# Attention beside a gated feed-forward on one core: value products in blocks of eight key tiles, one token buffer refilled by chunks, half of v in DRAM

## The chip, the core and the metric

The kernel runs on one core of a Trainium2 chip. The metric is the device time of one execution in microseconds (us), lower is better. The kernel before took 1323.13 us (median of three runs, 1322.75 to 1323.53).

## What is computed

For 2048 tokens `x` of width 448, the output is a mix of two blocks with a gate for each token:

```
g   = sigmoid((x * gate_w).sum(-1))
a   = softmax(q k^T * 28**-0.5) v   for 16 heads of width 28,   then @ wo
b   = (relu(x @ W_gate) * (x @ W_up)) @ W_down                  width 1792
out = g * a + (1 - g) * b
```

All inputs and the output are float32.

## The kernel before, in words

**Precision.** Most products are split: an operand is rounded to the type F32R ("high", made on ScalarE, `act_high`) and the rest ("low", a subtraction on VectorE or GpSimd, `low` and `pool_low`) is kept as a second operand. A contraction over 448 becomes eleven matmuls, `TERMS`: pairs of a weight chunk and a token chunk, where chunks 0 to 3 of the tokens are the high parts and 4 to 7 the low parts. `BY_CHUNK` is the same eleven pairs, sorted so that all pairs on one quarter of the tokens stand together. Only the value products (`pv`) are plain float32; each shows in the trace as two matmuls.

**Stages.** All five engines have their order written out by hand; each engine does its instructions in program order, and waits where an operand or a buffer is not ready.

1. *Projections* (to about 152 us). `qk` and `vproj` make k, q and v from four token blocks of 512. k and q go to DRAM (`qk_d`); v stays in the tile `V` (line 104): 128 keys x 16 key tiles x 16 heads x 32, where column 28 holds ones, which gives the softmax sums. The tokens of blocks 1 to 3, high and low, go to DRAM (`x_d`, `spill_x`). They lie in slots that later hold other things: P slots (`p_slot`, line 107, five buffers) and a Q slot. Block 0 stays in the two buffers of `x_slot` (line 113).
2. *Attention and feed-forward together* (152 to 1030 us). The work is cut into 64 rounds. A round handles `PB = 4` of the 256 pairs of a head and a key tile, and has two parts. First an order string is walked letter by letter: `s` is one score matmul (line 164, 512 queries) and its exponential on ScalarE into a P slot (line 166); `m` is two matmuls of scores laid out the other way (line 138) and a maximum over them on VectorE (line 140), for a head about one and a half ahead; `x` is one of the eleven matmuls of a gate or up half of the feed-forward (`gu_mm`, line 374). Then comes a **block** of value products for the four pairs (`pv`, line 400): sixteen products on 32 columns of the array each, four side by side, which show as 32 matmuls. Rounds 0 to 57 use `ROUND` (16 s, 8 m, 11 x: 43 matmuls, as an m is two); rounds 58 to 63 use `LATE` (16 s, 22 x). After eleven x a half is complete: a gate half is taken by `relu` on ScalarE, an up half by `spill_h`, which multiplies on VectorE and sends the tile to DRAM.
3. *The rest* (from 1030 us): the remaining 22 of 56 gate/up tiles (`gate_up`, each 22 matmuls), 56 down products (`down`, 12 matmuls each) and 16 output projections (`wout`, 11 each), interleaved by the list `todo`.

**PSUM buffers around the change.** Scores have two buffers (`s`), so a score matmul needs the exponential of two before it to be done. Maxima have two (`mx`), so an m needs the maximum of two before it. Feed-forward halves have one (`x`) up to round 57, and use `mx` in LATE.

**Between rounds** come the smaller steps: loads of k and q for a later head (SyncE's queue), `smax_end` (one transpose on TensorE, line 148, two copies on ScalarE, one subtraction on VectorE, two DMAs on GpSimd's queue) once for each head, `row_sums`, `spread` and `normalise` for a finished head. After the string, and before the block, stand the splits of the next weights (`split_f`: ScalarE, GpSimd) and their loads (`fetch_f`, SyncE's queue).

**Feed-forward tokens.** Gate/up tiles 0 to 13 read token block 0, 14 to 27 block 1, and so on. Block 1 is loaded back from `x_d` at round 24 into two buffers of its own (`att_x`), block 2 at round 40 into the `x_slot` buffers, block 3 in the last stage into two more (`pf_x`).

Of the kernel before, what the change touches and what calls it, by code (L numbers as in the profile page):

```python
# [8 lines left out]
F32 = mybir.dt.float32  # L9
F32R = mybir.dt.float32r  # L10
# [8 lines left out]
P = 128  # L19
S = 2048  # L20
D = 448
H = 16
# [13 lines left out]

LEAD = 24

PB = 4

ROUND = "smsxxsmsxsmsxmsxsmsxxsmsxsmsxxsmsxs"

LATE = "sxsxxsxsxxsxsxxsxsxxsxsxxsxsxxsxsxsxsx"

# [9 lines left out]
def gated_mix_kernel(ctx, tc, x, wq, wo, wgu, wd, out):  # L56
# [8 lines left out]
    def f32(ap):  # L65
        return ap.bitcast(F32)
# [27 lines left out]

    x_d = {(tb, r): dram.tile([P, 4, TB], F32, name=f"x_d_{tb}_{r}") for tb in range(1, NB) for r in range(2)}

    l_d = [dram.tile([NB, TB], F32, name=f"l_d_{h}") for h in range(H)]
    o_d = dram.tile([D, S], F32, name="o_d")
    wo_d = dram.tile([D, D], F32, name="wo_d")
# [1 line left out]

    stk = ctx.enter_context(ExitStack())
    vp = stk.enter_context(tc.tile_pool(name="vp", bufs=1))
    V = vp.tile([P, NK, H, 32], F32, name="V")
    K = [vp.tile([P, S], F32R, name=f"K{r}") for r in range(3)]

    def p_slot(name, dt=F32):
        return vp.tile([P, 4, TB], dt, name=name, tag="P", bufs=PB + 1)

    def q_slot(name):  # L110
        return vp.tile([P, 4, TB], F32R, name=name, tag="Q", bufs=3)

    def x_slot(name):
        return keep.tile([P, 4, TB], F32R, name=name, tag="xf", bufs=2)

    Q = {}

    def load_k(h):
        for r in range(4):
            nc.sync.dma_start(f32(K[h % 3])[DH * r:DH * (r + 1)], qk_d[r % 2, 2 * DH * h:2 * DH * h + DH, :])  # L120

    def load_q(h):
        Q[h] = q_slot(f"Q_{h}").rearrange("p j t -> p (j t)")
        for r in range(4):
            nc.sync.dma_start(f32(Q[h])[DH * r:DH * (r + 1)], qk_d[r // 2, 2 * DH * h + DH:2 * DH * (h + 1), :])
# [33 lines left out]
    def scores(i, j):  # L159
        h, kt = divmod(i, NK)  # L160
        if j == 0:
            PT[i] = p_slot(f"P_{i}")
        ps = ps_s(f"s_{i}_{j}")
        nc.tensor.matmul(ps, K[h % 3][:GD + 2, kt * P:(kt + 1) * P], Q[h][:GD + 2, j * TB:(j + 1) * TB],  # L164
                         start=True, stop=True)
        nc.scalar.activation(PT[i][:, j], ps, AF.Exp, scale=SCALE)  # L166
# [3 lines left out]
    def xf(tb, b):  # L170
        return X[tb][b // 4][:, b % 4]


    with tc.tile_pool(name="qkv", bufs=1) as pa:
# [42 lines left out]
                r.append((c, c + step, part))  # L217
            return r

        slots = {0: (x_slot, x_slot), 1: (p_slot, p_slot), 2: (p_slot, p_slot), 3: (p_slot, q_slot)}  # L220

        def x_tiles(tb):
            X[tb] = tuple(f(f"X{r}_{tb}", F32R) if f is p_slot else f(f"X{r}_{tb}") for r, f in enumerate(slots[tb]))

        def split_x(tb, raw):
            for c0, c1, xr in raw:
# [21 lines left out]
        def vproj(tb, t):  # L248
            ps = ps_any(f"v_{tb}_{t}")
            for n, (a, b) in enumerate(TERMS):  # L250
                nc.tensor.matmul(ps[:, :VC], xf(tb, b)[:, t * P:(t + 1) * P], W[:, a, 2 * D:], start=(n == 0),  # L251
                                 stop=(n == NT - 1))
            k = tb * 4 + t
            nc.scalar.activation(V[:, k, :, :DH], ps[:, :D].rearrange("p (h d) -> p h d", d=DH), AF.Copy)
            nc.scalar.activation(zt[:, k:k + 1], ps[:, D:D + 1], AF.Copy)

        for tb in range(NB - 1, -1, -1):
            x_tiles(tb)
        w0 = load_w(0)
        x0 = load_x(0, 1)  # L260
        w1 = load_w(1)
# [12 lines left out]
        gate = const.tile([P, 2, NK], F32, name="gate")  # L274
        for k in K:
            nc.gpsimd.memset(f32(k)[96:128], -1.0)
        nc.gpsimd.memset(V[:, :, :, DH:], 0.0)
        nc.gpsimd.memset(V[:, :, :, DH:DH + 1], 1.0)

        split_first(w0[0], x0)  # L280
        split_w(*w1)
# [79 lines left out]
            low(w[64:, :, 6], wr[64:, :, 3], w[64:, :, 6])  # L361
            del WR[i]

    def att_x(name):
        return att.tile([P, 4, TB], F32R, name=name, tag=name[:3], bufs=1)

    def load_x_split(tb, slot):
        X[tb] = tuple(slot(f"XF{r}_{tb}") for r in range(2))
        for r in range(2):
            nc.sync.dma_start(f32(X[tb][r]), x_d[tb, r])  # L370

    def gu_mm(ps, i, s, n):
        a, b = TERMS[n]
        nc.tensor.matmul(ps, WS[i][:, s, a], xf(i // NF, b), start=(n == 0), stop=(n == NT - 1))  # L374

    RL = {}

# [17 lines left out]
    def pv(i):  # L395
        h, kt = divmod(i, NK)
        if kt == 0:
            PO[h] = ps_o(f"po_{h}")
        for j in range(NB):
            nc.tensor.matmul(PO[h][32 * j:32 * j + 32], V[:, kt, h], PT[i][:, j], start=(kt == 0), stop=(kt == NK - 1))  # L400
        del PT[i]
        if kt == NK - 1:
            OS[h] = fe.tile([P, TB], F32, name=f"os_{h}", tag="os", bufs=2)
            nc.scalar.activation(OS[h], PO.pop(h), AF.Copy)
            LS[h] = fe.tile([P, 16], F32, name=f"ls_{h}", tag="ls", bufs=2)
            nc.gpsimd.dma_start(LS[h], OS[h][DH::32].rearrange("j (p c) -> j p c", c=16))
# [19 lines left out]
    def pack_wo():  # L426

        for j in range(4):
            nc.sync.dma_start(wo_d.rearrange("(g j d) n -> j d g n", j=4, d=DH)[j], wo[32 * j:32 * j + DH])
# [13 lines left out]
        act_high(WO[:, 6], r[:, 3])  # L443
        pool_low(WO[64:, 6], r[64:, 3], WO[64:, 6])

    NR = NI // PB
    X_ROUNDS = {24: (1, att_x), 40: (2, x_slot)}
    LAST_M = (len(maxima) - 2 * LEAD) // 8

    nxt = parts = 0  # L450
    done = (LAST_M - 1 + 2 * (NR - LAST_M)) // 2

    fetch_f(0)
    fetch_f(1)
    load_k(2)
    load_q(2)
    scores(0, NB - 1)
    for r in range(NR):
        h, q = divmod(r, NK // PB)
        order = ROUND if r < LAST_M else LATE  # L460
        todo = list(range(nxt, min(nxt + (0 if r == 0 else 1 if r < LAST_M else 2), 2 * done)))
        nxt += len(todo)
        if r in X_ROUNDS:
            load_x_split(*X_ROUNDS[r])

        if q == 0 and h and h + 2 < H:
            load_k(h + 2)
            load_q(h + 2)
        if r == 1:
            gates()  # L470
        if r == 2:
            pack_wo()
        if r < LAST_M and m in range(2 * NK, len(maxima), 2 * NK):
            smax_end(m // (2 * NK) - 1)
        if r == LAST_M:
            smax_end(H - 1)
        if h and q == 1:
            row_sums(h - 1)
            spread(h - 1)
        if h and q == 2:  # L480
            normalise(h - 1)
        ns = nx = 0
        for o in order:
            if o == "s":
                i, j = PB * r + 1 + ns // NB, ns % NB
                if i < NI:
                    scores(i, j)
                ns += 1
            elif o == "m":
                smax(m)  # L490
                m += 1
            elif nx < NT * len(todo):
                i, half = divmod(todo[nx // NT], 2)
                if nx % NT == 0:
                    ps = ps_x(f"gu_{i}_{half}") if r < LAST_M else ps_w(f"gu_{i}_{half}")[:, 0]
                gu_mm(ps, i, half, nx % NT)
                nx += 1
                if nx % NT == 0:
                    (spill_h if half else relu)(i, ps)

        ready = min(nxt + (2 if r + 1 < LAST_M else 3), 2 * done + 2)
        while parts < ready:
            split_f(parts // 2, pool_low, (parts % 2,))
            parts += 1
            if parts % 2 == 0:
                fetch_f(parts // 2 + 1)
        if r == LAST_M:
            wor = load_wo()
        for i in range(PB * r, PB * (r + 1)):
            pv(i)  # L510
            if i == NI - NK // 2:
                split_wo(wor)
    stk.close()


# [17 lines left out]
    def wout(tb, t):  # L533
        if t % 2 == 0:
            GA[tb, t // 2] = ps_w(f"wo_{tb}_{t}")
        ps = GA[tb, t // 2]
        for n, (a, b) in enumerate(TERMS):
            nc.tensor.matmul(ps[:, t % 2, :D], ON[tb][b // 4][:, b % 4, t * P:(t + 1) * P], WO[:, a], start=(n == 0),  # L538
                             stop=(n == NT - 1))
        if t == 0:  # L540
            GA[tb] = pf.tile([P, 4, D], F32, name=f"ga_{tb}", tag="ga", bufs=1)
        if t % 2:
            for u in (t - 1, t):
                k = tb * 4 + u
                nc.vector.tensor_scalar(GA[tb][:, u], ps[:, u % 2, :D], gate[:, 0, k:k + 1], None, op0=OP.mult)
# [47 lines left out]
                                               op0=OP.mult, op1=OP.add)  # L593
                (nc.sync if tb == NB - 1 else nc.gpsimd).dma_start(out[k * P:(k + 1) * P, :], y)

    def pf_x(name):
        return pf.tile([P, 4, TB], F32R, name=name, tag=name[:3], bufs=1)


    todo = [(gate_up, done), (row_sums, H - 1), (gate_up, done + 1)]  # L600
    for i in range(NB * NF):
# [6 lines left out]
        todo[n:n] = new  # L608


    before(1, (spread, H - 1))
    before(3, (normalise, H - 1))
    for tb, load, split, i in ((0, 4, 6, 9), (1, 9, 11, 14), (2, 21, 24, 28), (3, 35, 38, 42)):
        before(load, (fetch_o, tb))
        before(split, (split_o, tb, 0))
        before(split + 1, (split_o, tb, 2))
        before(i, *((wout, tb, t) for t in range(4)))
    n = todo.index((gate_up, (NB - 1) * NF))
    todo[n - 4:n - 4] = [(load_x_split, NB - 1, pf_x)]

    for i in range(4):
        fetch_d(i)
# [46 lines left out]
```

## Time and profile before

| what | value |
|---|---|
| median of three runs | 1323.13 us |
| the profiled execution: its own time | 1323.03 us |
| its span in the trace | 1321.3 us |
| granted TensorE clock | 1.0 |
| stage 0 to 152 us: TensorE / VectorE / ScalarE busy | 148.5 / 100.7 / 52.6 us |
| stage 152 to 1029.8 us: TensorE / VectorE / ScalarE busy | 877.6 / 581.4 / 642.1 us of 877.8 |
| the same stage: DMA share, rate | 28%, 77 GB/s |
| stage 1029.8 us to the end: TensorE busy | 287.2 us of 291.5 |

Busy time of TensorE counts a matmul from its start to its modelled end; a matmul of 512 columns shows 395 ns, while the next one starts some 233 ns after it. So where a stream of matmuls is dense or not is read from the distance between starts, which the timeline gives, and not from the busy share. The weight loads of the matmuls are listed as an engine of their own, PEld.

### The profile page before, as it was taken

To read this page: it belongs to the slowest core of one execution; us is meant where nothing else is said; L and a number is where in the kernel's file an instruction comes from. 1 tells how busy PE (TensorE), PEld (TensorE's weight loads), DVE (VectorE), ACT (ScalarE), POOL (GpSimd) and SP (SyncE) were. 2 spreads that over 40 slices of the span, in tenths; PEclk is the share of its full clock that TensorE was granted. 3 is DMA by queue.
4 is the path that set the end of the run, shared out by engine and by line. 5 is a ranking of instruction groups with operands and counts; after the bars stand their busy time and mean duration, and the time that the engine had idled before them with its cause. 6 is when DMAs were issued, how large, how long until landed. Compare 5 with 4: busy or idle time off the path is not lost.

```text
span 1321.3 us, 17544 instructions
## 1 busy us (share of the span) xinstructions
PE 1313.3 (99%) x6689; PEld 894.3 (68%) x6689; DVE 815.3 (62%) x859; ACT 772.6 (58%) x1454; POOL 307.0 (23%) x434
## 2 busy tenths in 40 slices
PE   9999999999999999999999999999999999999998
PEld 5888656656656566566566566565655788888997
DVE  6567867767767767677677677677600456633342
ACT  5212667767767777777677677677788332322121
POOL 3111112131121212222221221312325332301120
PEclk9999999999999999999999999999999999999999
DMA  8744622313223151331324313231122674433432
GB/s 298 263 171 180 175 62 61 81 48 99 56 71 88 40 152 57 89 88 40 88 86 123 77 51 81 61 92 32 50 91 79 209 265 149 163 121 120 133 113 78
DMA packets 50013, 144.67 MB, mean 109 GB/s; under 512 B 9544, under 2 KB 16648, under 8 KB 44808
## 3 DMA queue, kind: packets, MB, share of 16 engines
q1 hardware_dynamic: 33640, 96.70, 25.5%
q0 software_dynamic: 16288, 46.84, 10.2%
q8 instruction: 53, 0.87, 0.3%
q14 instruction: 32, 0.26, 0.1%
HBM read 99.96 MB, written 43.93 MB: 109 GB/s over the span
## 4 chain that ended last, share of the span: by engine, by line
PE 98%; DMA 1%; ACT 0%; DVE 0%; issue 0%; SPq 0%; ACTq 0%
PE gu L374 22%; PE s L164 20%; PE sm L138 19%; PE po L400 17%; PE acc L586 10%; PE qk L242 4%; PE v L251 3%; PE wo L538 3%; DMA xr<-x 1%; DMA qk_d<-st 1%; PE mt L148 0%; ACT X L81 0%; DVE X L87 0%; ACT st L81 0%; ACT P L166 0%
## 5 line engine op out<-in xcount | busy, mean ns | idle before, releaser
L140 DVE TENSOR_REDUCE mx<-sm 128x1 f32<-128x1024 f32 x512 | 606.5, 1219 | 174.9 <-PE sm L138 171.9
L166 ACT ACTIVATE P<-s 128x512 f32<-128x512 f32 x1024 | 583.1, 596 | 168.6 <-PE s L164 109.3
L164 PE MATMUL s<-Q,K 114*128 114x512 f32 x1024 | 419.5, 410 | 0.5 <-ACT P L166 0.5
L138 PE MATMUL sm<-K,Q 112*128 112x512 f32 x1024 | 323.4, 399 | 0.2
L164 PEld LDWEIGHTS s<-Q,K 114*128 114x128 f32 x1024 | 192.1, 188 | 146.8 <-ACT P L166 83.1
L374 PE MATMUL gu<-XF,wg 128*128 128x512 f32 x924 | 270.8, 395 | 0.0
L400 PE MATMUL po<-P,V 128*32 128x512 f32 x2048 | 233.0, 595 | 0.0
L138 PEld LDWEIGHTS sm<-K,Q 112*128 112x128 f32 x1024 | 189.6, 189 | 45.6 <-DVE mx L140 9.9
L374 PEld LDWEIGHTS gu<-XF,wg 128*128 128x128 f32 x924 | 174.6, 189 | 34.1 <-issue 0.8
L90 POOL TENSOR_TENSOR wg<-wgr,wg 128x384 fp32r<-128x384 f32 (+1 forms) x105 | 95.8, 914 | 283.3 <-ACT wg L81 187.5
L400 PEld LDWEIGHTS po<-P,V 128*32 128x32 f32 x2048 | 60.0, 109 | 131.0 <-issue 130.7
L586 PE MATMUL acc<-WD,hh 128*128 128x448 f32 x672 | 141.7, 367 | 0.0
L586 PEld LDWEIGHTS acc<-WD,hh 128*128 128x128 f32 x672 | 126.2, 188 | 12.8
L389 POOL DMA_DIRECT2D h_d<-h x56 | 31.4, 562 | 394.6 <-DVE h L383 188.4
L383 DVE TENSOR_TENSOR h<-gu,rl 128x512 f32<-128x512 f32 x56 | 38.4, 686 | 132.1 <-ACT rl L380 71.1
L380 ACT ACTIVATE rl<-gu 128x512 f32<-128x512 f32 x56 | 33.3, 594 | 128.0 <-PE gu L374 128.0
L374 PE MATMUL gu<-X,wg 128*128 128x512 f32 x308 | 108.0, 395 | 0.0
L87 DVE TENSOR_TENSOR hh<-hr,hh 128x512 fp32r<-128x512 f32 x56 | 55.3, 988 | 51.8 <-ACT hh L81 51.8
L81 ACT ACTIVATE hh<-hr 128x512 fp32r<-128x512 f32 x56 | 35.1, 628 | 74.3 <-PE acc L586 72.4
L242 PE MATMUL qk<-X,W 128*128 128x512 f32 x308 | 76.5, 398 | 1.9 <-ACT X L81 1.6
L81 ACT ACTIVATE wg<-wgr 128x384 fp32r<-128x384 f32 x168 | 72.6, 484 | 0.0
L242 PEld LDWEIGHTS qk<-X,W 128*128 128x128 f32 x308 | 57.4, 189 | 18.0 <-ACT X L81 2.6
(56 smaller groups left out, 596.6 us busy)
## 6 DMA issues: line engine op xcount, KB each, us to landing
wgr<-wgu SPq DMA_DIRECT2D x56, 512.0 KB
qk_d<-st POOLq DMA_DIRECT2D x28, 512.0 KB, 3.7
K<-qk_d SPq DMA_DIRECT2D x64, 224.0 KB
Q<-qk_d SPq DMA_DIRECT2D x64, 224.0 KB
h_d<-h POOLq DMA_DIRECT2D x56, 256.0 KB, 2.3
hr<-h_d SPq DMA_DIRECT2D x56, 256.0 KB
x_d<-X POOLq DMA_DIRECT2D x6, 1024.0 KB, 5.1
XF<-x_d SPq DMA_DIRECT2D x6, 1024.0 KB
```

What stands on the lines that cost most here:

```text
L81: nc.scalar.activation(dst, src, AF.Copy)
L87: nc.vector.tensor_tensor(dst, src, f32(high), op=OP.subtract)
L90: nc.gpsimd.tensor_tensor(dst, src, f32(high), op=OP.subtract)
L138: nc.tensor.matmul(ps[:, c, :], Q[h][:GD, u * P:(u + 1) * P], K[h % 3][:GD, k0:k0 + TB], start=True, stop=True)
L140: nc.vector.tensor_reduce(MX[h][:, 2 * u + half:2 * u + half + 1], ps, axis=AX.XY, op=OP.max)
L164: nc.tensor.matmul(ps, K[h % 3][:GD + 2, kt * P:(kt + 1) * P], Q[h][:GD + 2, j * TB:(j + 1) * TB], start=True, stop=True)
L166: nc.scalar.activation(PT[i][:, j], ps, AF.Exp, scale=SCALE)
L242: nc.tensor.matmul(ps, W[:, a, c * P:(c + 1) * P], xf(tb, b), start=(n == 0), stop=(n == NT - 1))
L251: nc.tensor.matmul(ps[:, :VC], xf(tb, b)[:, t * P:(t + 1) * P], W[:, a, 2 * D:], start=(n == 0), stop=(n == NT - 1))
L374: nc.tensor.matmul(ps, WS[i][:, s, a], xf(i // NF, b), start=(n == 0), stop=(n == NT - 1))
L400: nc.tensor.matmul(PO[h][32 * j:32 * j + 32], V[:, kt, h], PT[i][:, j], start=(kt == 0), stop=(kt == NK - 1))
L586: nc.tensor.matmul(ACC[tb][t][:, :D], hh[:, a, t * P:(t + 1) * P], WD[:, f, b], start=(f == 0 and n == 0), stop=(f == NF - 1 and n == 2))
```

## The change

- The order strings are new. Two rounds of four pairs (`SHORT`, the old `ROUND`; the first without x, the second with one half) are followed by 28 rounds of **eight** pairs: 25 of `LONG` (32 s, 16 m, 33 x: 97 matmuls, three halves), in runs of nine, eight and eight, and after each run one of `WIDE` (32 s, 16 m, 44 x: 108 matmuls, four halves). Six rounds of `LATE` follow as before. So there are 36 blocks instead of 64, and 100 halves (50 gate/up tiles) in this stage instead of 68 (34 tiles); the last stage keeps 6 `gate_up` instead of 22.
- Nine P slots (`NP = 9`) instead of five. Two of them (5 and 6) lie in the tile `V`, which is laid out by groups of four heads now: the last two groups, heads 8 to 15, are sent to DRAM (`v_d`) as they are made, by eight DMAs on GpSimd's queue, and loaded over the first two groups when heads 0 to 3, and 4 to 7, are done (SyncE's queue, at pairs 64 and 128).
- The feed-forward's tokens have one pair of buffers. `gu_mm` goes by `BY_CHUNK`; in the last up half of a token block, when the last matmul on a quarter of the tokens has been issued, two DMAs on SyncE's queue load this quarter of the next block over it. The three separate loads and their buffers go.
- The small steps between rounds are called every four pairs as before, so every second time in the middle of a string.
- In the last stage, `spread`, `normalise`, the loads and splits of the attention output and `wout` stand at other places of the list, and `ga` has two buffers.

```diff
-PB = 4
-ROUND = "smsxxsmsxsmsxmsxsmsxxsmsxsmsxxsmsxs"
+SHORT = "smsxxsmsxsmsxmsxsmsxxsmsxsmsxxsmsxs"
+LONG = "ssmmxsxxsxsmxxsxsmsxxsxxsmmsxxsxxsxsmsxxsmsmsxsxxsxmsmsxxxxsmxssxxmsxsmsxxsmsxmss"
+WIDE = "msxxsmsxsxmsxxsxmsxxxxmssmxsxxsxxsmxmssxxxxsxsmsmsxxxxsxsmsxmsxxsxxxsmsmxxxsxsxxxsxmssxmxxss"
 LATE = "sxsxxsxsxxsxsxxsxsxxsxsxxsxsxxsxsxsxsx"
+ROUNDS = [(SHORT, 0), (SHORT, 1)] + [(LONG, 3)] * 9 + ([(WIDE, 4)] + [(LONG, 3)] * 8) * 2 + [(WIDE, 4)] + [(LATE, 2)] * 6
+NP = 9
...
+    v_d = {g: dram.tile([P, NK, 4, 32], F32, name=f"v_d_{g}") for g in (2, 3)}
...
-    V = vp.tile([P, NK, H, 32], F32, name="V")
+    V = vp.tile([P, 4, NK, 4, 32], F32, name="V")
-    def p_slot(name, dt=F32):
-        return vp.tile([P, 4, TB], dt, name=name, tag="P", bufs=PB + 1)
+    def p_slot(k, name, dt=F32):
+        if k in (5, 6):
+            return V[:, k - 3].rearrange("p k h d -> p (k h d)").rearrange("p (j t) -> p j t", t=TB)
+        return (vp if k < 5 else att).tile([P, 4, TB], dt, name=name, tag=f"P{k}", bufs=1)
...
+            if t == 3:
+                for g in (2, 3):
+                    nc.gpsimd.dma_start(v_d[g][:, k - 3:k + 1], V[:, g, k - 3:k + 1])
...
-        nc.gpsimd.memset(V[:, :, :, DH:], 0.0)
-        nc.gpsimd.memset(V[:, :, :, DH:DH + 1], 1.0)
+        for g in range(G):
+            nc.gpsimd.memset(V[:, g, :, :, DH:], 0.0)
+            nc.gpsimd.memset(V[:, g, :, :, DH:DH + 1], 1.0)
...
+    for tb in range(1, NB):
+        X[tb] = X[0]
     def gu_mm(ps, i, s, n):
-        a, b = TERMS[n]
+        a, b = BY_CHUNK[n]
         nc.tensor.matmul(ps, WS[i][:, s, a], xf(i // NF, b), start=(n == 0), stop=(n == NT - 1))
+        c = b % 4
+        if i % NF == NF - 1 and s and i < NB * NF - 1 and (n == NT - 1 or BY_CHUNK[n + 1][1] % 4 != c):
+            for r in range(2):
+                nc.sync.dma_start(f32(X[0][r])[:, c], x_d[i // NF + 1, r][:, c])
...
+    def small_things(u):
+        h, q = divmod(u, 4)
+        if q == 0 and h and h + 2 < H:
+            load_k(h + 2)
+            load_q(h + 2)
+        if u in (16, 32):
+            g = u // 16 + 1
+            nc.sync.dma_start(V[:, g % 2], v_d[g])
...
+        if h and q == 1:
+            row_sums(h - 1)
+            spread(h - 1)
+        if h and q == 2:
+            normalise(h - 1)
...
-    for r in range(NR):
+    for r, (order, nu) in enumerate(ROUNDS):
+        ni = order.count("s") // NB
...
+        small_things(i0 // 4)
+        if m % (2 * NK) == 0 and i0 <= NI - LEAD:
             smax_end(m // (2 * NK) - 1)
...
+                i, j = i0 + 1 + ns // NB, ns % NB
+                if ns == 4 * NB:
+                    small_things(i0 // 4 + 1)
...
-        for i in range(PB * r, PB * (r + 1)):
+        for i in range(i0, i0 + ni):
             pv(i)
...
-    before(1, (spread, H - 1))
-    before(3, (normalise, H - 1))
-    for tb, load, split, i in ((0, 4, 6, 9), (1, 9, 11, 14), (2, 21, 24, 28), (3, 35, 38, 42)):
+    before(0, (spread, H - 1))
+    before(1, (normalise, H - 1))
+    for tb, load, split, at in ((0, 2, 3, (4, 5, 6, 7)), (1, 5, 8, (10, 11, 14, 14)), (2, 21, 24, (28,) * 4),
+                                (3, 35, 38, (42,) * 4)):
```

More of the change, by code (lines that the diff above doesn't have):

```diff
@@ L113, in x_slot @@
     def x_slot(name):
-        return keep.tile([P, 4, TB], F32R, name=name, tag="xf", bufs=2)
+        return keep.tile([P, 4, TB], F32R, name=name, tag=name[:2], bufs=1)
     Q = {}
@@ L161, in scores @@
         if j == 0:
-            PT[i] = p_slot(f"P_{i}")
+            PT[i] = p_slot(i % NP, f"P_{i}")
         ps = ps_s(f"s_{i}_{j}")
@@ L218, in load_x @@
             return r
-        slots = {0: (x_slot, x_slot), 1: (p_slot, p_slot), 2: (p_slot, p_slot), 3: (p_slot, q_slot)}
-        def x_tiles(tb):
-            X[tb] = tuple(f(f"X{r}_{tb}", F32R) if f is p_slot else f(f"X{r}_{tb}") for r, f in enumerate(slots[tb]))
+        X[0] = tuple(x_slot(f"X{r}") for r in range(2))
+        free = iter(range(5))
+        for tb in range(NB - 1, 0, -1):
+            X[tb] = tuple(q_slot(f"X{r}_{tb}") if tb + r == NB else p_slot(next(free), f"X{r}_{tb}", F32R)
+                          for r in range(2))
         def split_x(tb, raw):
@@ L253, in vproj @@
             k = tb * 4 + t
-            nc.scalar.activation(V[:, k, :, :DH], ps[:, :D].rearrange("p (h d) -> p h d", d=DH), AF.Copy)
+            nc.scalar.activation(V[:, :, k, :, :DH], ps[:, :D].rearrange("p (g h d) -> p g h d", g=G, d=DH), AF.Copy)
             nc.scalar.activation(zt[:, k:k + 1], ps[:, D:D + 1], AF.Copy)
-        for tb in range(NB - 1, -1, -1):
-            x_tiles(tb)
+            if t == 3:
+                for g in (2, 3):
+                    nc.gpsimd.dma_start(v_d[g][:, k - 3:k + 1], V[:, g, k - 3:k + 1])
         w0 = load_w(0)
@@ L362, in split_f @@
             del WR[i]
[L364 to L370, printed above, removed]
+    for tb in range(1, NB):
+        X[tb] = X[0]
     def gu_mm(ps, i, s, n):
-        a, b = TERMS[n]
+        a, b = BY_CHUNK[n]
         nc.tensor.matmul(ps, WS[i][:, s, a], xf(i // NF, b), start=(n == 0), stop=(n == NT - 1))
+        c = b % 4
+        if i % NF == NF - 1 and s and i < NB * NF - 1 and (n == NT - 1 or BY_CHUNK[n + 1][1] % 4 != c):
+            for r in range(2):
+                nc.sync.dma_start(f32(X[0][r])[:, c], x_d[i // NF + 1, r][:, c])
     RL = {}
@@ L399, in pv @@
         for j in range(NB):
-            nc.tensor.matmul(PO[h][32 * j:32 * j + 32], V[:, kt, h], PT[i][:, j], start=(kt == 0), stop=(kt == NK - 1))
+            nc.tensor.matmul(PO[h][32 * j:32 * j + 32], V[:, h // 4 % 2, kt, h % 4], PT[i][:, j], start=(kt == 0),
+                             stop=(kt == NK - 1))
         del PT[i]
@@ L444, in split_wo @@
         pool_low(WO[64:, 6], r[64:, 3], WO[64:, 6])
[L446 to L451, printed above, removed]
+    done = sum(n for _, n in ROUNDS) // 2
+    nxt = parts = i0 = 0
+    def small_things(u):
[6 more added lines that the diff above has]
+            nc.sync.dma_start(V[:, g % 2], v_d[g])
+        if u == 1:
+            gates()
+        if u == 2:
+            pack_wo()
+        if h and q == 1:
[3 more added lines that the diff above has]
+            normalise(h - 1)
     fetch_f(0)
@@ L457, in gated_mix_kernel @@
     scores(0, NB - 1)
-    for r in range(NR):
[L459 to L473, printed above, removed]
-            smax_end(m // (2 * NK) - 1)
[L475 to L481, printed above, removed]
+    wor = None
+    for r, (order, nu) in enumerate(ROUNDS):
+        ni = order.count("s") // NB
+        late = "m" not in order
+        todo = list(range(nxt, nxt + nu))
+        nxt += nu
+        small_things(i0 // 4)
+        if m % (2 * NK) == 0 and i0 <= NI - LEAD:
+            smax_end(m // (2 * NK) - 1)
+        if late and wor is None:
+            wor = load_wo()
         ns = nx = 0
@@ L484, in gated_mix_kernel @@
             if o == "s":
-                i, j = PB * r + 1 + ns // NB, ns % NB
+                i, j = i0 + 1 + ns // NB, ns % NB
+                if ns == 4 * NB:
+                    small_things(i0 // 4 + 1)
                 if i < NI:
@@ L491, in gated_mix_kernel @@
                 m += 1
-            elif nx < NT * len(todo):
+            elif nx < NT * nu:
                 i, half = divmod(todo[nx // NT], 2)
                 if nx % NT == 0:
-                    ps = ps_x(f"gu_{i}_{half}") if r < LAST_M else ps_w(f"gu_{i}_{half}")[:, 0]
+                    ps = ps_w(f"gu_{i}_{half}")[:, 0] if late else ps_x(f"gu_{i}_{half}")
                 gu_mm(ps, i, half, nx % NT)
@@ L499, in gated_mix_kernel @@
                     (spill_h if half else relu)(i, ps)
-        ready = min(nxt + (2 if r + 1 < LAST_M else 3), 2 * done + 2)
+        ready = nxt + (ROUNDS[r + 1][1] if r + 1 < len(ROUNDS) else 2)
+        ready += ready % 2
         while parts < ready:
@@ L506, in gated_mix_kernel @@
                 fetch_f(parts // 2 + 1)
-        if r == LAST_M:
-            wor = load_wo()
-        for i in range(PB * r, PB * (r + 1)):
+        for i in range(i0, i0 + ni):
             pv(i)
@@ L512, in gated_mix_kernel @@
                 split_wo(wor)
+        i0 += ni
+    assert i0 == NI and m == len(maxima), (i0, m)
     stk.close()
@@ L540, in wout @@
         if t == 0:
-            GA[tb] = pf.tile([P, 4, D], F32, name=f"ga_{tb}", tag="ga", bufs=1)
+            GA[tb] = pf.tile([P, 4, D], F32, name=f"ga_{tb}", tag="ga", bufs=2)
         if t % 2:
@@ L594, in down @@
                 (nc.sync if tb == NB - 1 else nc.gpsimd).dma_start(out[k * P:(k + 1) * P, :], y)
-    def pf_x(name):
-        return pf.tile([P, 4, TB], F32R, name=name, tag=name[:3], bufs=1)
     todo = [(gate_up, done), (row_sums, H - 1), (gate_up, done + 1)]
@@ L616, in gated_mix_kernel @@
         before(split + 1, (split_o, tb, 2))
-        before(i, *((wout, tb, t) for t in range(4)))
-    n = todo.index((gate_up, (NB - 1) * NF))
-    todo[n - 4:n - 4] = [(load_x_split, NB - 1, pf_x)]
+        for t, i in enumerate(at):
+            before(i, (wout, tb, t))
     for i in range(4):
```

## The prediction

> **What bounds the kernel now.** I read the page first. TensorE is busy 99% of the span, and the chain that ended last runs on it for 98%; ScalarE and VectorE stand at 58% and 62%. But a busy share does not say that matmuls follow each other as closely as they can, so I then read the timeline of TensorE by the starts of its matmuls, around one round of the long middle stage:
>
> ```profile
> PE   9999999999999999999999999999999999999998
> ...
> PE 98%; DMA 1%; ACT 0%; DVE 0%; issue 0%; SPq 0%; ACTq 0%
> ```
> ```profile
> 599.81 0.40 PE L164 MATMUL s<-Q,K 114*128 114x512 f32 x1
> 600.13 3.64 PE L400 MATMUL po<-P,V 128*32 128x512 f32 x32
> 603.71 0.50 PE L164 MATMUL s<-Q,K 114*128 114x512 f32 x1
> 604.05 0.62 PE L138 MATMUL sm<-K,Q 112*128 112x512 f32 x2
> 604.51 0.40 PE L164 MATMUL s<-Q,K 114*128 114x512 f32 x1
> 604.74 0.63 PE L374 MATMUL gu<-XF,wg 128*128 128x512 f32 x2
> 605.21 0.40 PE L164 MATMUL s<-Q,K 114*128 114x512 f32 x1
> ```
> Columns: start, duration, engine, line, names, shape, count. Full-width matmuls start 0.23 us apart (604.05 to 604.51 for two, 604.74 to 605.21 for two). I call 0.233 a slot. The same timeline for weight loads shows the block:
> ```profile
> 602.31 0.13 PEld L400 LDWEIGHTS po<-P,V 128*32 128x32 f32 x4 [0.30 <-issue]
> 602.74 0.13 PEld L400 LDWEIGHTS po<-P,V 128*32 128x32 f32 x4 [0.30 <-issue]
> 603.70 0.19 PEld L164 LDWEIGHTS s<-Q,K 114*128 114x128 f32 x1 [0.84 <-issue]
> 603.81 0.43 PEld L138 LDWEIGHTS sm<-K,Q 112*128 112x128 f32 x2
> ```
> Inside the block four products go side by side every 0.43 us, eight such groups: 3.43 us. The first score load after it comes at 603.70, with nothing loaded ahead while the block ran.
>
> **The price of a block's two edges.** From the last s before it (599.81) to the second matmul after it (604.05) are 4.24 us. Two slots and eight groups would be 0.47 + 3.43 = 3.90. So 0.34 us go at the edges: 600.13 - 599.81 is 0.32 where a slot is 0.23; the s after the block takes 604.05 - 603.71 = 0.34; the rest lies at the block's first weights and its last drain.
>
> **What is left of a round.** Blocks start at 600.13 and 614.04: 13.91 us. Less 43 slots (10.02), 3.43 and 0.34 there remain 0.12 us of stalls, where an s waits for the exponential of two before. Rounds with the transpose are longer, 614.04 to 628.31: 14.27, so 0.36 more, 0.03 of it the transpose; 0.33 are m that wait for VectorE, which has two other jobs first:
> ```profile
> 618.57 0.28 DVE L87 TENSOR_TENSOR mh<-mr,mh 16x128 fp32r<-16x128 f32 x1 [3.70 <-ACT mh L152]
> 618.78 0.67 DVE L422 TENSOR_TENSOR os<-os,rb 128x512 f32<-128x512 f32 x1
> 619.38 5.73 DVE L140 TENSOR_REDUCE mx<-sm 128x1 f32<-128x1024 f32 x5
> ```
> Five reduces back to back take 5.73, so one comes every 1.13 us, and eight fill 9.1 of the 10.0 us outside the block: 91%. Exponentials back to back start 0.495 us apart (606.36 and 606.85): sixteen fill 79%. A LATE round is 13.05 us (989.68 to 1002.73): less 38 slots (8.85), 3.43 and 0.34 it stalls 0.43. The last round, with twelve s and eleven x, takes 10.45 (1015.78 to 1026.23) and stalls 1.32, as its last s have no x between them. The stage after 1030 us has starts 0.234 (gate/up) and 0.205 (down) apart, no stall to speak of.
>
> **The change, part by part.** The profiled execution took 1323.03 us beside a span of 1321.3, and the median shown is 1323.13; I sum against 1323.03. The matmuls are the same in number and shape, so slots and groups cancel, also those of the 16 gate/up tiles that move into the middle stage.
>
> 1. *Edges.* 64 blocks become 36: 28 x 0.34 = **-9.5 us**.
> 2. *Stalls of the strings.* The 56 rounds replaced stall 56 x 0.12 + 13 x 0.33 = 11.0 (of the 14 with a transpose, the first has no `normalise` and does not stall). For the new strings I count places where PSUM is short. An s needs the end of the exponential of two before: 0.43 to its start, 0.60 for it, 0.16 until the matmul streams, 1.19 us or 5.1 slots. ROUND has six spans of three s in 5 slots, so 0.02 us each. LONG, for twice the pairs, has nine: 0.18; WIDE five: 0.10. Their halves end where at most two s stand in the next five slots, so the relu finds room. 25 x 0.18 + 3 x 0.10 = 4.8. With a transpose, the first reduce starts 1.77 us late (617.61 to 619.38) and ends at 2.97; LONG's third m stands at slot 13 (3.03) and needs 2.97 + 0.16, a stall of 0.10; the fourth has room: 13 x 0.10 = 1.3. Average loads fall too: reduces 16 x 1.13 in 22.6 us, 80%; exponentials 70%. Together 6.1, so **-4.9 us**. From both sides: no stall left, -11.0; as dense as LATE, which loses 0.43 per 38 slots, 25 x 1.10 + 3 x 1.22 = 31, so +20. The likely end is the near one, as LONG has one s per 0.71 us against 0.55 in LATE.
> 3. *LATE.* Before, it starts with an odd half: the one that ends in mid-string goes to VectorE, the relu falls into the block (ScalarE's relu at 976.91, the block from 976.54). Now it starts even, and the relu, 0.495 of ScalarE's time, falls in mid-string, where ScalarE goes from 7.9 to 8.4 of 8.85 us. Between 0 and 0.5 a round; 0.3, five times: **+1.5 us**.
> 4. *Last round.* Eleven more x stand between its s; of 1.32 I keep 0.4: **-0.9 us**. Bounds -1.3 and 0.
> 5. *Token quarters.* Each is 512 KB in two DMAs on SyncE's queue, behind a matmul. Halves 28, 56 and 84 start with WIDE, so a block (8 x 0.86 = 6.9 us) and WIDE's first three slots stand between. The first quarter is free 28 slots before the block's edge, so it has 14 us; the last, four slots before it, has 13 until its matmul. Four quarters are 2.1 MB, 7 us at the 299 GB/s of the first 40 us. Hidden: 0. Without that cover it would cost some 2 to 5 us at each of three places (a 256 KB spill lands in 2.3, a 1 MB spill in 5.1). SyncE's queue waits meanwhile for the matmuls; behind it are weights fetched a round ahead, and k and q of a head first used 28 us later.
> 6. *v in DRAM.* Eight more issues on GpSimd's queue (about 0.56 us each, as for `h_d`) before 152 us, where GpSimd is busy 32 of 152 us; two 1 MB loads on SyncE's queue, needed 64 pairs (some 240 us) later. The smaller memsets end at latest four times later than now (6.2 us from 6.71), when GpSimd's next issue at 12.46 is due. The exponential of pair 5 waits for the last spill of v, over a round old. 0; at worst a spill's 5 us once.
> 7. *Splits and the last stage.* 32 more half splits on GpSimd (1.01 + 0.36) and ScalarE lie in the 6.9 us blocks, at most four at a time: ScalarE 2.9, GpSimd 5.5 us. In the last stage downs follow each other with fewer gate/up tiles between. Each needs 0.99 + 0.46 of VectorE, 1.24 of GpSimd and 480 KB in 2.46 us while weights come in, 195 GB/s against the 299 seen. The output projections between the downs add room. 0; at worst 0.5 at each of ten downs, 5 us.
>
> Sum: 1323.03 - 9.5 - 4.9 + 1.5 - 0.9 = **1309.2 us**, 1.05% less.
>
> **Rivals.**
> *The edges stay.* If what I read as edges were paid for every group or every pair (weights not loaded ahead at all), fewer blocks would save nothing: 1309.2 + 9.5 = 1318.7. Against it: groups inside the block keep 0.43 with loads of 0.13 hidden, and s loads of 0.19 run under other matmuls (603.81 to 605.69). The Trainium skill (TensorE: Matmul & The Clock Gate, part 3, The mechanism) says that a weight load overlaps running matmuls only when the row group differs; all matmuls here use the same rows, so by it no load is ever hidden and a switch costs nothing special. The trace disagrees, at a slot of 0.233 with a load of 0.19. Chance 0.06.
> *The strings bite.* ScalarE or VectorE falls behind in the middle of the longer strings. At no gain in stalls the time is 1314.1, at LATE's density 1334. Slower than before only from 0.7 us a round. For it: runs like `xxmmss`, and small steps that now fall in mid-string; against it the loads above. Chance 0.10.
> *Quarter by quarter is not what happens (slower).* If a matmul on a quarter must wait until the load of another quarter of the same buffer has landed, TensorE stops at three places in each of three changes of block, nine times 2.3 to 5.1 us: +21 to +46, so 1330 to 1355. It decides from 1.5 us a stop. Against it: at the start TensorE reads the first quarter at 6.48 while VectorE still writes the last until 10.1, in the same two buffers. Chance 0.07.
>
> **The numbers.** The forecast has 0.77, from 1304 (stalls gone) to 1315. To hold 8 in 10, with item 7's worst, the range is 1303 to 1318. A run of this kernel can tell about 0.2%, 2.6 us, from no change. Faster: 0.77, 0.04 of the first rival, 0.07 of the second: 0.88. Within 0.2%: 0.02 of each of these two, 0.04. Slower: 0.01 of the second and 0.07 of the third: 0.08.
>
> **What would show it.** In the middle stage: blocks of 64 matmuls with 0.43 between groups throughout and one s load 0.84 after the last; rounds of LONG near 22.6 + 6.87 + 0.34 + 0.2 = 30.0 us, the same within 0.2 with a transpose; no gap at the first x of WIDE; LATE near 13.35. Wrong are the steps if LONG exceeds 30.6, if gaps stand between x on different quarters, or if the last stage shows starts more than 0.24 apart.

## The result, and the profile after

The changed kernel takes 1314.82 us (median of six runs, 1311.76 to 1316.39) against 1323.33 us of the kernel before on the same chips: ratio 0.9934, 95% interval 0.9921 to 0.9947. The forecast was 1309.2 (1303 to 1318). Its runs lie 4.6 us apart, those of before 1 us. The profiled execution took 1315.21 us, span 1313.4.

The page after, its chain of work:
```profile
PE 93%; DMA 3%; issue 1%; DVE 1%; POOL 1%; ACT 1%; SPq 0%; POOLq 0%; ACTq 0%; DVEq 0%
```
The chain ran on TensorE for 98% before; now other engines have 7% of it, and that is new. TensorE's timeline around a block of the middle stage, and the weight loads at its end:
```profile
403.49 0.65 PE L173 MATMUL s<-Q,K 114*128 114x512 f32 x2
404.06 3.64 PE L413 MATMUL po<-P,V 128*32 128x512 f32 x32
407.52 1.90 PE L413 MATMUL po<-V 128*32 128x512 f32 x16
409.24 1.90 PE L413 MATMUL po<-P,V 128*32 128x512 f32 x16
411.07 0.28 PE L157 MATMUL mt<-ident,m 128*16 128x128 f32 x1
411.10 0.70 PE L173 MATMUL s<-Q,K 114*128 114x512 f32 x2
```
```profile
409.67 0.13 PEld L413 LDWEIGHTS po<-P,V 128*32 128x32 f32 x4 [0.30 <-issue]
410.10 0.13 PEld L413 LDWEIGHTS po<-P,V 128*32 128x32 f32 x4 [0.30 <-issue]
411.07 0.09 PEld L157 LDWEIGHTS mt<-ident,m 128*16 128x16 f32 x1 [0.84 <-issue]
```
64 products run as one block (the rows named `po<-V` read the P slots that lie in `V`), in steps of 0.43 us to the end, and the 0.84 us without a weight load comes once. Blocks start at 404.06 and 434.05: a round of LONG is 30.0 us.

By stages, from the traces of the two profiled executions (82.3 us is 352 matmuls of the moved gate/up tiles at 0.234):

| stretch | before, us | after, us | difference without the moved matmuls |
|---|---|---|---|
| start to first block | 152.6 | 153.6 | +1.0 |
| first block to last value product | 876.7 | 943.5 | 66.8 - 82.3 = -15.5 |
| to the end of the last matmul | 287.7 | 210.4 | -77.3 + 82.3 = +5.0 |
| from there to the end of the span | 4.3 | 5.9 | +1.6 |

The four stretches add up to -7.9 us, the difference of the two spans. The middle stage gained more than forecast (-13.8); the last stage, costed at nothing, lost 5. Its timeline on TensorE, and on GpSimd:
```profile
1138.56 0.97 PE L558 MATMUL wo<-WO,on 128*128 128x448 f32 x4
1140.36 1.29 PE L558 MATMUL wo<-WO,on 128*128 128x448 f32 x5 [0.82 <-ACT on L85]
1143.38 0.67 PE L558 MATMUL wo<-WO,on 128*128 128x448 f32 x2 [1.74 <-POOL on L94]
```
```profile
1135.69 1.16 POOL L94 TENSOR_TENSOR WD<-wdr,WD 128x448 fp32r<-128x448 f32 x1
1140.38 0.56 POOL L402 DMA_DIRECT2D h_d<-h  x1 [3.53 <-DVE WD L88]
1140.96 2.36 POOL L94 TENSOR_TENSOR on<-or,on 128x1024 fp32r<-128x1024 f32 x1
```
The first output projection stops twice and waits for the second half of the split `on`: first for ScalarE's part, then for GpSimd's. GpSimd's part is 2.4 us, and stands in its queue behind the spill of gate/up tile 55. GpSimd is idle for 3.53 us ahead of that spill, because the tile's product is made only after its last matmul, which runs just before the projection. (VectorE makes the product at 1139.39; the row names the cast of down weights that VectorE does right behind it, and which ends at 1140.38.) A third, shorter gap stands at a projection of token block 1. The three gaps (1.18, 2.10, 0.94 us) and the slow starts behind them come to 3.9 us over the plain spacing; another 0.9 of the 5.0 is that down matmuls start 206.5 ns apart and not 205.2, of which the cause stays open.

The theory to be tried: the middle stage gains 0.33 us for each block that goes, and some 5 to 6 us of stalls by the spacing of the letters (this second part did not hold as it stands, as the point-by-point part shows); the shortfall is the order in GpSimd's queue. The rivals: the price goes by products and not by blocks; the gain came from the additional halves as filler; the shortfall comes from v's transfers.

### The profile page after: what moved, and what is told of

Read it like the earlier page. It is cut to its first block, busy times and chain, and to the rows that moved or that the text cites. A ratio compares the mean times of both kernels' runs of the same rounds, so it can differ in the third digit from the quotient of the medians.

```text
span 1313.4 us, 17652 instructions
## 1 busy us (share of the span) xinstructions
PE 1300.0 (99%) x6689; PEld 907.0 (69%) x6689; DVE 799.4 (61%) x811; ACT 770.5 (59%) x1454; POOL 360.8 (27%) x496
## 4 chain that ended last, share of the span: by engine, by line
PE 93%; DMA 3%; issue 1%; DVE 1%; POOL 1%; ACT 1%; SPq 0%; POOLq 0%; ACTq 0%; DVEq 0%
PE gu L383 21%; PE s L173 19%; PE sm L147 18%; PE po L413 17%; PE acc L606 10%; PE qk L253 3%; PE wo L558 3%; PE v L262 2%; DMA K<-qk_d 1%; DMA qk_d<-st 1%; POOL on L94 1%; DMA wr<-wq 0%; DMA xr<-x 0%; DMA wdr<-wd 0%; PE mt L157 0%
## 5 line engine op out<-in xcount | busy, mean ns | idle before, releaser
L175 ACT ACTIVATE P<-s 128x512 f32<-128x512 f32 x800 | 455.0, 597 | 111.1 <-PE s L173 76.1
L173 PE MATMUL s<-Q,K 114*128 114x512 f32 x1024 | 400.7, 405 | 0.4 <-ACT P L175 0.3
L383 PE MATMUL gu<-X,wg 128*128 128x512 f32 x1232 | 397.0, 396 | 0.0
L147 PE MATMUL sm<-K,Q 112*128 112x512 f32 x1024 | 312.2, 396 | 0.7 <-DMA K<-qk_d 0.5
L383 PEld LDWEIGHTS gu<-X,wg 128*128 128x128 f32 x1232 | 233.5, 190 | 43.9 <-issue 0.8
L413 PE MATMUL po<-P,V 128*32 128x512 f32 x1600 | 181.9, 594 | 0.0
L94 POOL TENSOR_TENSOR wg<-wgr,wg 128x384 fp32r<-128x384 f32 x153 | 142.2, 941 | 99.8 <-issue 48.7
L175 ACT ACTIVATE V<-s 128x512 f32<-128x512 f32 x224 | 128.2, 598 | 33.2 <-PE s L173 21.2
L413 PEld LDWEIGHTS po<-P,V 128*32 128x32 f32 x1600 | 49.1, 110 | 110.5 <-issue 110.5
L413 PE MATMUL po<-V 128*32 128x512 f32 x448 | 54.1, 594 | 0.0
```

The costliest lines, as they stand in the source:

```text
L94: nc.gpsimd.tensor_tensor(dst, src, f32(high), op=OP.subtract)
L147: nc.tensor.matmul(ps[:, c, :], Q[h][:GD, u * P:(u + 1) * P], K[h % 3][:GD, k0:k0 + TB], start=True, stop=True)
L413: nc.tensor.matmul(PO[h][32 * j:32 * j + 32], V[:, h // 4 % 2, kt, h % 4], PT[i][:, j], start=(kt == 0), stop=(kt == NK - 1))
```

## The experiments

**e1**: the last stage's list, projections of block 0 later.
```diff
-    for tb, load, split, at in ((0, 2, 3, (4, 5, 6, 7)), (1, 5, 8, (10, 11, 14, 14)),
+    for tb, load, split, at in ((0, 2, 3, (6, 7, 8, 9)), (1, 6, 10, (14, 14, 14, 14)),
```


> The changed kernel with the last stage's list altered alone: the output projections of token block 0 stand before downs 6, 7, 8, 9 (they stood before 4 to 7), the load of block 1's attention output before down 6 (5), its splits before 10 and 11 (8 and 9), its projections all before 14. Theory A (the missing microseconds are TensorE waiting at the projections for GpSimd, whose split stands behind the spill of a feed-forward tile that is not made yet): the three gaps of 1.18, 2.10 and 0.94 us in the changed kernel's last stage go, 3.9 us with their after-effects: 1314.8 - 3.9 = 1310.9. Rival (GpSimd's work is too much for this stretch wherever it stands, and the wait comes back at the downs): 1314 to 1315.


1311.34 us, ratio 0.9907 (0.9891 to 0.9922). The three gaps are gone, but down 13 waits 1.7 us: its split of the last weights (1.6 us on GpSimd) stood behind two splits of `on` (2.55 us each).

**e8**: the same with block 1's splits at 12 in place of 10.


> The changed kernel with the last stage's list altered as in e1, but the splits of block 1's attention output before downs 12 and 13 (e1 had 10 and 11, and down 13 waited 1.7 us for GpSimd's split of the last down weights, which stood behind two splits of 2.5 us). Theory A: no gap over 0.4 us in the last stage, 1314.8 - 3.9 = 1310.9 or a little less, 1.7 below e1. Rival (the work of GpSimd is too much here): a gap again, at downs 14 to 16.


1308.99 us, ratio 0.9890 (0.9876 to 0.9905). From the last value product to the last matmul 206.5 us instead of 210.4, no gap over 0.1 above the plain spacing behind the first gate/up matmul. These 3.9 us of the shortfall were queue order, not GpSimd's load.

**e2** and **e3**: the blocks cut, strings as changed. The edit of e2 is shown; e3 does the same after 8, 16 and 24 of the s, with two pairs each time.
```diff
                 if ns == 4 * NB:
                     small_things(i0 // 4 + 1)
+                    for p in range(i0, i0 + 4):
+                        pv(p)
...
-        for i in range(i0, i0 + ni):
+        for i in range(i0 + (4 if ni == 8 else 0), i0 + ni):
             pv(i)
```


> The changed kernel with each block of eight pairs cut in two: the products of the first four pairs stand in the middle of the string, after sixteen of its s. Strings, slots, halves, buffers all as changed; 64 blocks again instead of 36. Theory A (an edge pair costs 0.34 us for each block): +28 x 0.34 = +9.5, less at most 0.2 us a round of stalls that the pause in mid-string lets ScalarE and VectorE make good (28 x 0.2 = 5.6): 1318.7 to 1324.3, nearest 1323. Rival B (the price goes by groups or pairs, and the gain came from the strings): 1314.8, within 1.


1322.82 us, ratio 0.9994 (0.9985 to 1.0002): all of the gain is gone. The middle stage takes 952.7 us instead of 943.5: 9.1 us for 28 blocks, 0.33 each (round by round 0.28 to 0.35, and one of 0.78).

> The same with blocks of two pairs in the 28 long rounds (after 8, 16, 24 and all s): 120 blocks. Theory A: 84 x 0.34 = +28.6 over the changed kernel, less up to 5.6: 1337.8 to 1343.4, and the step from blocks of four is twice that from eight to four. Rival B: 1314.8, within 1. A third way, a price that grows when the engines get less time to empty their buffers: over 1345.


1353.85 us, ratio 1.0229 (1.0215 to 1.0243): the third way. The middle stage is 984.5 us, 41.0 more than as changed; 84 blocks at 0.33 are 27.5, and 13.4 are something else. ScalarE and TensorE of this kernel, after the last block of a round:
```profile
199.76 2.37 ACT L85 ACTIVATE wg<-wgr 128x384 fp32r<-128x384 f32 x6
202.02 0.59 ACT L418 ACTIVATE os<-po 128x512 f32<-128x512 f32 x1
202.50 2.99 ACT L175 ACTIVATE P<-s 128x512 f32<-128x512 f32 x5
```
```profile
202.27 0.40 PE L383 MATMUL gu<-X,wg 128*128 128x512 f32 x1
203.15 0.50 PE L173 MATMUL s<-Q,K 114*128 114x512 f32 x1 [0.48 <-ACT P L175]
```
The six weight splits, which had lain in a block of 6.9 us, now overrun one of 1.7 us; the exponentials start at 202.50, and TensorE waits. This is what the block covers, and what it costs without that cover: the step to the next block is 8.65 to 8.67 us behind six splits instead of 7.91 behind three, in 12 of the 28 rounds: 9.0 of the 13.4. Rounds that show no such wait are 0.96 to 0.99 longer than as changed, again 0.32 to 0.33 for each of three blocks.

**e4**: v stays in SBUF, without its spills and loads.
```diff
-            if t == 3:
-                for g in (2, 3):
-                    nc.gpsimd.dma_start(v_d[g][:, k - 3:k + 1], V[:, g, k - 3:k + 1])
...
-            nc.sync.dma_start(V[:, g % 2], v_d[g])
+            pass
```


> The changed kernel without the eight spills of v to DRAM and the two loads back; heads 8 to 15 then use the values of heads 0 to 7, which leaves out part of the computation. Theory A (these transfers are hidden): 1314.8, within 1. Rival C (the extra 4 MB of transfers delay the projections' own loads, where the changed kernel starts its first block 1.0 us later): 1313.8 or less, with the first block at 152.6 us instead of 153.6.


1313.43 us, ratio 0.9923 (0.9909 to 0.9936), and the changed kernel had 0.9921 to 0.9947: no difference that can be told. Its first block starts at 152.9 us; over the thirteen traces of this study that start lies between 152.0 and 154.2, with no order by this change. So the +1.0 of the table is spread between executions.

**e6** and **e9**: blocks of eight without the additional halves, both with the last stage's list of e8.
```diff
-ROUNDS = [(SHORT, 0), (SHORT, 1)] + [(LONG, 3)] * 9 + ([(WIDE, 4)] + [(LONG, 3)] * 8) * 2 + [(WIDE, 4)] + [(LATE, 2)] * 6
+ROUNDS = [(SHORT, 0), (SHORT, 1)] + [(SHORT + SHORT, 2)] * 28 + [(LATE, 2)] * 5 + [(LATE, 1)]
```


> Blocks of eight pairs with the strings of before: each long round is the old string twice (32 s, 16 m, 22 x, two halves), so 68 halves and 34 tiles stand in the middle stage as before the change, and 22 in the last stage; the last stage's list is that of e8. Theory A (an edge pair is 0.34 us whatever the strings): 1323.4 - 28 x 0.34 = 1313.9, with rounds of 86 slots at 20.04 + 6.86 + 0.34 + 0.24 = 27.5 us, and 0.33 more in those with a transpose. If the stalls of the strings were as large a part as the prediction says, the changed kernel's middle stage is 4.9 us better than this one for the same matmuls. Rival (the gain came from the strings and the filler): 1320 or more, rounds of 27.8.


1335.75 us, ratio 1.0095 (1.0080 to 1.0110): slower than both, and the expectation missed twice. Its rounds take 28.0 us, not 27.5: at the joint of the two strings three s stand in 3 slots, and each time the s waits. And at tile 14 this happened on SyncE's queue and on TensorE:
```profile
534.10 1.64 SPq L129 DMA_DIRECT2D K<-qk_d  x4
535.85 3.56 SPq L134 DMA_DIRECT2D Q<-qk_d  x4
540.56 10.49 SPq L387 DMA_DIRECT2D X<-x_d  x8
```
```profile
547.22 0.39 PE L173 MATMUL s<-Q,K 114*128 114x512 f32 x1
551.27 1.19 PE L383 MATMUL gu<-X,wg 128*128 128x512 f32 x2 [3.66 <-DMA X<-x_d]
```
Here halves 27 and 28 meet in mid-string, with no block between, and the loads of the token quarters are issued just behind 1.8 MB of k and q. The round is 5.2 us longer than its neighbours. At the next change of tokens (halves 55 and 56, also in mid-string, when no more k and q are loaded) no gap shows; in the last stage tile 42 stopped for 4.8 us in all. One more thing stands in these rounds, which have the old letters: the usual ones take 27.99 to 28.04 us with a transpose and 27.95 to 28.11 without, where before the change a round with a transpose took 0.4 us more.

> e6 mended in two places. Its round was the old string twice, and at the joint three s stand in 3 slots, which lost 0.5 us a round; here the long round has the same 32 s, 16 m and 22 x in an order without such a joint (16 spans of three s in 5 slots, none shorter). And the quarters of tokens are not loaded back, so all gate/up tiles read token block 0, which leaves out part of the computation. Theory A: rounds of 20.04 + 6.86 + 0.33 + about 0.25 = 27.5 us; 1323.2 - 28 x 0.33 (edges) - 2.7 (stalls, mostly those of the transpose rounds) = 1311.3, with 22 gate/up tiles in the last stage as before the change. Rival (the gain hung on the additional halves as filler): 1319 or more, rounds of 27.8.


```diff
-LONG = "ssmmxsxxsxsmxxsxsmsxxsxxsmmsxxsxxsxsmsxxsmsmsxsxxsxmsmsxxxxsmxssxxmsxsmsxxsmsxmss"
+LONG = "smsxxsmsxxsmsxsmsxsmsxsmsxsmsxsxxsmsmxsxsmsxxsmsxsmsxxsmsmsxxsxsmsmxss"
```
1315.69 us (1311.95 to 1316.94), ratio 0.9938 (0.9925 to 0.9952). The usual round is 27.44 to 27.56 us, as worked out. Six of the 28 run 0.2 to 1.1 longer, 3.2 us together, in the profiled execution, which took 1313.09. In each of the six VectorE waits 0.3 to 1.1 us for the DMA of a head's row sums, and the m queue up behind it; the longest:
```profile
320.71 0.25 DVE L421 RECIPROCAL rs<-ls 128x16 f32<-128x16 f32 x1 [1.09 <-DMA ls<-os]
```
The same wait makes one LONG round near 940 us 0.4 to 1.6 us longer in the traces of e1, e5, e7, e8, e10 and e11; that of the changed kernel has none. Why that DMA comes late in some executions, and why e9's runs lie 5 us apart and 4 above the sum in the median, stays open. The gain of long blocks stands without the filler: a usual round without a transpose takes 27.46, where two rounds of before take 27.80, 0.34 more for the one block more.

**e5**: the relu of LATE on VectorE.
```diff
-                    (spill_h if half else relu)(i, ps)
+                    (spill_h if half else relu_v if late else relu)(i, ps)
...
+        nc.vector.tensor_scalar(RL[i], ps, 0.0, None, op0=OP.max)
```


> The changed kernel, with the relu of the gate halves in the six LATE rounds made on VectorE (a maximum with 0) in place of ScalarE. Theory A, item 3 of the prediction (LATE lost 0.3 us a round because the relu now falls in mid-string on ScalarE): LATE rounds go from 13.32 us to 13.05 or less, as they were before the change, down to 12.75 if ScalarE with exponentials alone has room: 1.4 to 3 us less, 1314.8 - 2 = 1312.8. Rival (LATE stalls on something that the relu has no part in): 13.32 stays.


1312.39 us, ratio 0.9912 (0.9895 to 0.9928). LATE blocks of the changed kernel start at 1055.31 and 1068.63, 13.32 us apart; here 13.05, the value of before.

**e7**: e5 and e8 together.


> Both repairs together, e5 and e8: 1314.8 - 3.9 (gaps at the projections) - 2 (LATE) = 1308.9; it should also vary less from run to run than the changed kernel, where a gap of over 3 us at the projections is followed in some executions by a stretch of half clock.


1306.52 us (1305.40 to 1307.43), ratio 0.9872 (0.9857 to 0.9887).

**e10** and **e11**: other orders of the same letters, then LATE in blocks of eight.
```diff
+LONG = "smsmxsxxsxxsmsxxsmsxxsxxsmsmxsxsmxsxsmxsxsmxsxsxxxsmsmxsxsmxsxsxmsxsmxsxxsmsxxsms"
+WIDE = "smsxxmssxxxxxsxxsmsxxsmsmxsxsxxxsmmxssxxmxssxxmsmsxxxsxsmxxsxsxxmssxxmsmsxxxxssxmxmssxxxxxss"
...
-    [(LATE, 2)] * 6
+    [(LATE + LATE, 4)] * 3
```


> e7 with other orders for the same letters in LONG and WIDE: no span of three s in 5 slots (LONG has nine, WIDE five), halves still followed by six slots without an x. Theory A (what a long round stalls, 0.2 us, is these spans): rounds of 22.60 + 6.86 + 0.33 = 29.8 us instead of 30.0; 1306.5 - 25 x 0.2 - 3 x 0.13 = 1301.1. Rival (the 0.2 us belongs to the edges or to the slots): rounds of 30.0 stay, 1306.5.


1303.10 us, ratio 0.9850 (0.9836 to 0.9863). Two blocks of e10 one round apart:
```profile
341.55 1.92 PE L417 MATMUL po<-P,V 128*32 128x512 f32 x16
...
371.35 1.92 PE L417 MATMUL po<-P,V 128*32 128x512 f32 x16
```
29.8 us, where e7 has 29.97: without spans of three s in 5 slots a round is slots, groups and one pair of edges, 22.60 + 6.86 + 0.33 = 29.79. One round, with the wait for row sums, takes 31.11: 1.3 of what the kernel is above its expected 1301.1.

> e10 with the six LATE rounds joined to three of eight pairs (the string twice, four halves). Theory A: 3 fewer blocks, -1.0 us, and up to 0.3 us a round of new stalls, since the pause of a block comes only every 76 slots and ScalarE has 16 exponentials in 8.85 us: 1300.1 to 1301.1. Rival (the pause is what lets ScalarE keep up in LATE): 1302 or more.


1302.12 us, ratio 0.9841 (0.9827 to 0.9854), not apart from e10. Two LATE strings with one block take 26.1 us, just twice 13.05: the edges saved came back as s that wait, as the rival had it. e10 and e11 are faster than both kernels of the change.

## Why the prediction was right or wrong, point by point

- *Edges, -9.5*: right. 0.33 a block by e2, -9.1; e9 has them without the filler. The rival by which a switch costs nothing special is out. Products and other matmuls differ in two things, 32 columns against 128 and float32 against F32R, and no run separates them. The Trainium skill (TensorEngine Tiling (Array Packing), Key Properties) says that a change of tiling mode drains the array; the traces fit that, with 0.84 us without a weight load after each block, and add the price.
- *Stalls of the strings, -4.9*: the number came near, but most of it came another way than the prediction had it. The terms as measured (-9.1, +1.4, -0.9) leave -6.9 of the -15.5. Of these, 5.1 are the rounds with a transpose: 13 of them took 14.26 to 14.34 us before, where the others took 13.90, and in the changed kernel LONG takes 29.98 to 30.01 with a transpose and 29.99 to 30.02 without. The prediction kept VectorE's first reduce 1.77 us late in these rounds and let the new letters make up for all but 0.10 of it. What it overlooked is that the change also swaps two calls: `normalise`, now in `small_things`, comes ahead of `smax_end`, and came behind it before. VectorE around the transpose of 411.07:
```profile
405.63 1.52 DVE L436 TENSOR_TENSOR os<-os,rb 128x512 f32<-128x512 f32 x1 [0.30 <-DMA rb<-l_d]
412.02 0.28 DVE L91 TENSOR_TENSOR mh<-mr,mh 16x128 fp32r<-16x128 f32 x1 [4.87 <-ACT mh L161]
412.30 2.36 DVE L149 TENSOR_REDUCE mx<-sm 128x1 f32<-128x1024 f32 x2
```
The multiplication of `normalise` (`os`) now runs in the block, and the reduces start right behind `mh`, 1.23 us after the transpose. That it is this step, and not the letters, shows in two places: the one transpose round of before that has no `normalise` took 13.94, and e6, with the old letters in long blocks and the calls in the new order, has no difference either. No run turns the order back alone. The spacing of the letters is left with about 1.8 us; that spans of three s in 5 slots cost what the count says, 0.2 a round, e10 shows (30.0 to 29.8).
- *LATE, +1.5*: right, 13.05 to 13.32 in five rounds, +1.4; e5 shows that the relu is the cause.
- *Last round, -0.9*: right: 10.45 to 12.11 with eleven more x at 0.233 (2.56).
- *Token quarters, 0*: right; no gap at the first x of WIDE. The price without the cover was put at 2 to 5 us at each of three places; e6 had 5.2 (with k and q ahead in the queue), 0 and 4.8. The rival by which quarters wait for each other is out: the first loads are issued at 427.34, and x on the other quarters start in their places at 428.32 and 429.04, when all DMAs of the core together had moved 0.13 MB since, and the first quarter alone is 0.5 MB.
- *v in DRAM, 0*: right by e4, within what it can tell.
- *Last stage, 0*: this step failed. It set GpSimd's work against the time ("The output projections between the downs add room. 0"), and in the stretch there is time enough, as e8 shows. What it did not do is name what stands ahead of the moved split in GpSimd's queue: the spill of a tile that is not made yet. The projections had come after down 8, now they come after down 3, right behind the last gate/up tile, and the second half of the split right ahead of them. Its worst case, 5 us, was of the right size, but for downs.
- *The small steps in mid-string* were named for the second rival and given no price. They have one in some executions, VectorE's wait for row sums: 3.2 us in e9's trace, 1.3 in e10's, none in that of the changed kernel.
- The +1.6 us after the last matmul stay open as to cause: over the thirteen traces this end is 3.6 to 5.9 us, for the same four output DMAs.
- *The sum*: that 1314.82 lies in the range is in part luck. The range reached to 1318 for the sake of stops at the downs, which did not come, and the 1.7 us that the middle stage gained beyond the forecast hide a part of the 7.6 lost in the other three stretches.

## What to carry to other kernels

Where full-width matmuls and products on 32 columns alternate, count the changes, not only the products: each pair of changes cost 0.33 us here, and longer blocks also cover the steps of other engines, until the buffers run dry elsewhere. Space the letters of an order by what a buffer's turn needs (here three s in at least 6 slots); this gave about 1.8 us here, beside 9.1 from the edges. Put a step whose operand is ready ahead of one that waits on the same engine (5.1 us here, by one call moved). When a step is moved earlier, walk the queue of each engine that it uses, and ask of every instruction ahead of it when its own operand is made.

## What the runs showed of the hardware that was not expected

Gaps at the projections cost more than their length in some executions. The windows of e4's trace (columns: stretch, length, busy time and count of five engines, granted clock, DMA share, GB/s):
```profile
1138.00:1141.00 3.00, 1.37 (x6) 0.86 (x5) 2.53 (x3) 1.37 (x2) 2.05 (x2) 1.00 0.23 87
1141.00:1144.00 3.00, 2.08 (x6) 1.87 (x7) 2.51 (x1) 0.00 (x0) 1.95 (x2) 0.66 0.29 70
1144.00:1148.00 4.00, 4.00 (x18) 3.64 (x17) 0.00 (x0) 0.63 (x1) 0.00 (x0) 0.83 0.92 307
```
and the same stretch of the changed kernel's:
```profile
1138.00:1141.00 3.00, 2.18 (x11) 1.60 (x10) 1.13 (x3) 2.06 (x3) 0.59 (x2) 1.00 0.00 0
1141.00:1144.00 3.00, 1.26 (x7) 0.83 (x6) 3.00 (x1) 0.00 (x0) 3.00 (x2) 1.00 0.23 87
1144.00:1148.00 4.00, 4.00 (x21) 3.65 (x20) 0.98 (x1) 0.63 (x1) 0.42 (x1) 1.00 0.83 261
```
Both have the same gaps, 1.18 and 2.10 us; in e4 the clock falls behind the second (0.66 and 0.83; in finer windows 1.00 up to 1141.9, 0.51 from there to 1145.4, and 1.00 again), and nine matmuls start 0.373 us apart instead of 0.205, 1.5 us in all. e2 and e3 show it too, the changed kernel and e5 do not. That is 0.49 of 3.5 us lost; if the clock was half, the slow stretch is an estimated 3.4 us. In e6 such a stretch (0.51 from 550.9 to 554.4) follows the stop at tile 14, and is a part of its 5.2 us. The Trainium skill (TensorE: Matmul & The Clock Gate, Part 1) describes a free-running activity window of about 3.4 us, and that the array falls to half clock after an idle one. The length agrees, and a window that runs free would fit that only three of the five executions with these gaps are met. But in e4 the array was not idle for 3.4 us, as five matmuls ran between the two gaps.

Every execution's mean clock is on record, to three places. e7, without the gaps, has 1.000 in all four runs, which lie 2.0 us apart; e2's eleven go from 1320.36 us at 1.000 to 1325.38 at 0.996. The changed kernel's six have 0.999 or 1.000, so this may be a part of why they lie further apart, but it is not shown. It does not explain e9's, which have 1.000 in all five.
